# PReLU of a block pair: two loops over the pair, or one loop that alternates ScalarE and VectorE

## The chip, the cores and the metric

The kernel runs on one core of a Trainium2 chip. The metric is the device time of one execution, in microseconds. Three runs of the kernel before gave 373.78, 374.03 and 374.71 us, so the median is 374.03 us. The profiled execution took 374.39 us, and the span that its trace covers is 372.4 us. The TensorE clock was granted in full in it (mean 1.00).

## The reference

Two stages are chained. The first is a state-space scan (Mamba-2 SSD) over 4 batches, 8 heads and 768 tokens in chunks. Its result, laid out as 3072 tokens by 256 features, is the input of a feed-forward block with a PReLU:

```python
h = x @ w_in                                            # 3072 x 256 by 256 x 2048
g = np.maximum(h, 0.0) + alpha * np.minimum(h, 0.0)     # alpha: one slope per column, 2048
return (g @ w_out).astype(np.float32)                   # 3072 x 2048 by 2048 x 256
```

Everything is float32. The slope is a value per hidden feature, and hidden features lie on partitions in the kernel, so PReLU of a tile is two elementwise instructions with a scalar per partition. The first writes `alpha * h`; the second writes `max(s * h, that)` over it, where `s` is 1 or -1 (the sign is minus for slopes over 1, and is taken out again through the weights).

## The kernel before, in words

**Tiling.** The 3072 tokens are six groups of 512. A group's tokens come from two pairs of SSD chunks (`ssm`, `pair`, lines 416 to 637), which end in the tile `xT`. Group 0 goes through the feed-forward block plainly, tile by tile, while weights arrive (`hidden`, `output`, lines 643 to 688). Groups 1 to 5 use a seven-product scheme for a 2 by 2 block product instead of eight products, on both matrix products. One step of it is a *quad* (`quad`, line 760): four tiles of 128 hidden features, that is two row blocks of two tiles each, by 512 tokens, that is two column blocks of 256. There are four quads in a group, so twenty in all, from about 82 us to 361 us of the span.

**A quad.** Two PSUM tiles of one bank each, `A` and `Y` (name `hp`, pool `ps_h`, two buffers), receive the seven products of `x` with `w_in`. `first` (line 770) makes one product as two matmuls, one per half of the bank: half `p` = 0 and half `p` = 1. Between the products ScalarE and VectorE copy and add, so that four blocks result: `g12` from `Y` (line 799), `g22` from `c22` in SBUF (lines 800 and 802), `g21` from `A` (line 808), and `g11` from `Y` again (line 812). Each block is 128 partitions by two halves of 256, and PReLU is applied half by half because the two halves have different slopes. GpSimd then forms the block differences `tc_` (line 806) and `ta`, `tb`, `td` (line 815) from the four blocks. The copy of line 801 writes `m1` back into `Y` before the last product is added to it.

**The order around it.** The order of the work is written out by hand: nothing is rescheduled. `after(j)` is called between the steps of a quad and puts other work there for TensorE: the seven output products of the quad before (`product`, line 736), and the stages of the next SSD pairs (`ssm`). Every engine takes its instructions in the order in which the source issues them. Waits between engines are put in from the tiles that instructions read and write. For a PSUM bank an instruction also waits for another engine that uses any part of the bank; for an SBUF tile only for what touches the same part.

**The SSD pairs.** The pairs of groups 2 to 5 are worked in the quads of the group before. In every quad with `z` = 0 or 2 of groups 1 to 4 (eight quads, called *even* below), `after(13)` places the products of `products_bc` (line 563). They are eight matmuls into four PSUM tiles, `r` = 0 to 3, first for chunk 0 and then for chunk 1. Tiles `r` = 2 and `r` = 3 are taken by `spare` from the pool `ps_h`, so they take over the banks of `A` and `Y` of the running quad. VectorE multiplies them into `dec` (line 606). Between `g21` and `g11` VectorE also has the state updates (`states`, line 532) in these quads; ScalarE has a copy of the state (line 529) or a copy for the group's result (line 834) there in some of them.

The next quad takes the two `hp` buffers over in the same way: its `A` follows the old `A` (or tile `r` = 2), its `Y` the old `Y` (or tile `r` = 3).

Of the kernel before, what the change touches and what calls it, by code (L numbers as in the profile page):

```python
# [12 lines left out]
ALU = mybir.AluOpType  # L13
# [9 lines left out]
def kernel(  # L23
# [25 lines left out]
    nc = tc.nc  # L49
# [250 lines left out]
    s_mul = const.tile([P, NF], F32, name="s_mul")  # L300
    s_alpha = const.tile([P, NF], F32, name="s_alpha")
# [449 lines left out]
    def prelu(o, h, z, i, by=(nc.scalar, nc.vector)):  # L751

        fs = [slice(4 * z + 2 * p + i, 4 * z + 2 * p + i + 1) for p in range(2)]
        for p in range(2 if nc.scalar in by else 0):
            nc.scalar.mul(o[:, p], h[:, p], s_alpha[:, fs[p]])  # L755
        for p in range(2 if nc.vector in by else 0):
            nc.vector.scalar_tensor_tensor(out=o[:, p], in0=h[:, p], scalar=s_mul[:, fs[p]],  # L757
                                           in1=o[:, p], op0=ALU.mult, op1=ALU.max)

    def quad(g, z, after):  # L760

# [35 lines left out]
        first(Y, lambda q: s4[:, q], b22)  # L797
        g12, g22, g21, g11 = (tile_of(gp, "gt", "gt") for i in range(4))
        prelu(g12, Y, z, 0)
        prelu(g22, c22, z, 1, (nc.scalar,))  # L800
        nc.scalar.copy(out=Y, in_=m1)
        prelu(g22, c22, z, 1, (nc.vector,))
        after(7)
        after(8)
# [284 lines left out]
```

## Time and profile before

| | |
|---|---|
| median of three runs | 374.03 us |
| span of the trace | 372.4 us |
| TensorE busy | 365.4 us, 98% |
| VectorE busy | 243.1 us, 65% |
| GpSimd busy | 201.1 us, 54% |
| ScalarE busy | 179.7 us, 48% |
| line 755 on a PSUM half (ScalarE) | 120 instructions, mean 470 ns |
| line 757 on a PSUM half (VectorE) | 120 instructions, mean 479 ns |
| line 755 and 757 on an SBUF half | 40 each, mean 504 and 498 ns |

Busy time is the time in which an engine had at least one instruction in work. Where two instructions of one engine follow each other without a wait, the second starts before the end of the first is recorded, so a pair takes less than two single ones. The view in order of time merges such runs: it gives the start of the first, the time that the run covers, and the number of instructions; in brackets it gives the idle time before it and what ended that. Line numbers are those of the kernel before; in the kernel after, lines behind the change are one higher.

### The profile page before, as it was taken

The numbers are of one execution on the slowest core, as the hardware profiler recorded it, in microseconds if no ns is written. First come the engines' busy times: TensorE is split into PE (matmuls) and PEld (weight loads), VectorE is DVE, ScalarE is ACT, GpSimd is POOL, SyncE is SP. The second block draws the span as 40 slices with busy tenths as digits, with TensorE's granted clock in tenths as the row PEclk, the third lists the DMA queues.
The fourth block names the chain that finished last, engine by engine and source line by source line (L and its number), as shares of the span: only waits on it lengthen the run. The fifth ranks groups of instructions, "written<-read, shape, count | busy, mean of one in ns | idle before, by whom it ended". The sixth has DMA issues, their size and how long they took to land.

```text
span 372.4 us, 6183 instructions
## 1 busy us (share of the span) xinstructions
PE 365.4 (98%) x2223; PEld 295.1 (79%) x2223; DVE 243.1 (65%) x462; ACT 179.7 (48%) x384; POOL 201.1 (54%) x211
## 2 busy tenths in 40 slices
PE   8989999999999999999999999999999999999996
PEld 8766666578788888788788788788788788888884
DVE  7897979976448548738638847637848644643364
ACT  1647866435355355444444445445535525553541
POOL 4775565778929754724644525555445355264512
PEclk9999999999999999999999999999999999999999
DMA  7889999911176301005603703702801001001004
GB/s 147 181 151 322 276 284 202 181 31 58 48 136 112 72 3 56 2 0 79 134 3 61 151 2 54 159 0 45 167 2 29 2 0 23 8 0 30 1 0 85
DMA packets 121878, 30.71 MB, mean 82 GB/s; under 512 B 93736, under 2 KB 117752, under 8 KB 121848
## 3 DMA queue, kind: packets, MB, share of 16 engines
q1 hardware_dynamic: 116736, 29.74, 36.0%
q10 hardware_dynamic: 5112, 0.59, 1.1%
q8 instruction: 17, 0.28, 0.3%
q14 instruction: 13, 0.11, 0.1%
HBM read 26.98 MB, written 3.34 MB: 81 GB/s over the span
## 4 chain that ended last, share of the span: by engine, by line
PE 86%; DVE 10%; DMA 2%; issue 1%; ACT 1%; POOLq 0%; DVEq 0%; SPq 0%
PE hp L772 34%; PE bank L747 32%; PE bank L686 4%; DVE dec L438 3%; PE hp L648 2%; PE ss L629 2%; PE ss L570 2%; DMA rows<-in_a_dram 2%; DVE wr L239 1%; PE hp L270 1%; PE ss L622 1%; DVE dec L432 1%; PE hp L570 1%; DVE gt L652 1%; PE ss L520 1%; PE hp L663 1%
## 5 line engine op out<-in xcount | busy, mean ns | idle before, releaser
L815 POOL TENSOR_TENSOR gt<-gt 128x512 f32<-128x512 f32 x58 | 73.6, 1268 | 30.8 <-DVE gt L757 23.9
L757 DVE SCALAR_TENSOR_TENSOR gt<-hp,s_mul,gt 128x256 f32<-128x256 f32 x120 | 52.5, 479 | 46.9 <-ACT gt L755 45.9
L747 PE MATMUL bank<-gt,w_out 128*128 128x256 f32 x320 | 82.4, 382 | 0.0
L755 ACT ACTIVATE gt<-hp,s_alpha 128x256 f32<-128x256 f32 x120 | 50.3, 470 | 46.7 <-PE hp L772 32.5
L747 PEld LDWEIGHTS bank<-gt,w_out 128*128 128x128 f32 x320 | 60.1, 190 | 10.4 <-issue 2.3
L806 POOL TENSOR_TENSOR gt<-gt 128x512 f32<-128x512 f32 x20 | 25.4, 1270 | 78.8 <-DVE gt L757 78.8
L747 PE MATMUL bank<-gt,ws 128*128 128x256 f32 x240 | 58.3, 379 | 0.0
L747 PEld LDWEIGHTS bank<-gt,ws 128*128 128x128 f32 x240 | 45.1, 190 | 5.8
L438 DVE TENSOR_TENSOR_SCAN dec<-abc,bank 128x256 f32<-128x256 f32 x80 | 48.1, 660 | 0.0
L772 PE MATMUL hp<-xs,w_in 128*128 128x256 f32 x160 | 42.9, 390 | 0.0
L772 PE MATMUL hp<-xT,w_in 128*128 128x256 f32 x160 | 41.9, 384 | 0.0
L772 PE MATMUL hp<-xs,ws 128*128 128x256 f32 x160 | 41.1, 379 | 0.0
L791 DVE TENSOR_TENSOR hp<-hp,u 128x512 f32<-128x512 f32 x20 | 14.0, 700 | 39.8 <-ACT u L789 39.8
L780 ACT COPY m<-hp 128x512 f32<-128x512 f32 x20 | 11.7, 586 | 51.8 <-PE hp L772 51.8
L772 PEld LDWEIGHTS hp<-xs,w_in 128*128 128x128 f32 x160 | 28.7, 189 | 7.7 <-issue 3.0
L772 PEld LDWEIGHTS hp<-xs,ws 128*128 128x128 f32 x160 | 30.4, 190 | 4.1
L772 PEld LDWEIGHTS hp<-xT,w_in 128*128 128x128 f32 x160 | 29.7, 190 | 5.0 <-issue 1.4
L686 PE MATMUL bank<-w_out,gt 128*128 128x256 f32 x128 | 31.0, 384 | 0.0
L686 PEld LDWEIGHTS bank<-w_out,gt 128*128 128x128 f32 x128 | 23.7, 190 | 6.6 <-issue 3.7
L795 DVE TENSOR_TENSOR c<-hp,m 128x512 f32<-128x512 f32 x20 | 13.6, 681 | 19.3 <-PE hp L772 19.3
L648 PE MATMUL hp<-xT,w_in 128*128 128x512 f32 x48 | 22.8, 597 | 0.4 <-DVE gt L652 0.2
L789 ACT COPY u<-hp 128x512 f32<-128x512 f32 x20 | 11.7, 585 | 22.5 <-PE hp L772 22.5
(156 smaller groups left out, 555.4 us busy)
## 6 DMA issues: line engine op xcount, KB each, us to landing
abc<-z SPq DMA_DIRECT2D x20, 512.0 KB, 5.0
raw<-in_moe_w_in_dram SPq DMA_DIRECT2D x8, 512.0 KB, 5.0
raw<-in_moe_w_out_dram SPq DMA_DIRECT2D x8, 512.0 KB, 6.9
xt<-in_x_dram SPq DMA_DIRECT2D x24, 128.0 KB, 2.8
out_dram<-o_sb SPq DMA_DIRECT2D x32, 64.0 KB, 1.9
nat<-in_B_dram SPq DMA_DIRECT2D x22, 64.0 KB, 3.3
nat<-in_C_dram SPq DMA_DIRECT2D x22, 64.0 KB, 2.7
ap<-pf SPq DMA_DIRECT2D x11, 128.0 KB
```

Of the source, the lines that this page charges most:

```text
L438: nc.vector.tensor_tensor_scan(out=dv[:, k, hs], data0=abc[k][:, hs], data1=ident_p[0], initial=0.0, op0=ALU.mult, op1=ALU.add)
L648: nc.tensor.matmul(hp, w_in[:, k, f * P : (f + 1) * P], xts[g][:, k], start=(k == 0), stop=(k == KC - 1))
L686: nc.tensor.matmul(pos[0][t // 2][:, t % 2], gt[:, t * Q : (t + 1) * Q], w_out[:, f], start=(f == 0 and t % 2 == 0), stop=(f == NF - 1), s ...
L747: nc.tensor.matmul(ms[g][i][:, h], w, blocks[g, z][n][:, p], start=(q == 0 and h == 0), stop=(q == NQ - 1), skip_group_check=True)
L755: nc.scalar.mul(o[:, p], h[:, p], s_alpha[:, fs[p]])
L757: nc.vector.scalar_tensor_tensor(out=o[:, p], in0=h[:, p], scalar=s_mul[:, fs[p]], in1=o[:, p], op0=ALU.mult, op1=ALU.max)
L772: nc.tensor.matmul(to[:, p], w(2 * z + p), b, start=start and p == 0, stop=True, skip_group_check=True)
L780: nc.scalar.copy(out=m1, in_=A)
L791: nc.vector.tensor_tensor(out=Y, in0=Y, in1=u2, op=ALU.add)
L795: nc.vector.tensor_tensor(out=c22, in0=A, in1=m5, op=ALU.add)
L806: nc.gpsimd.tensor_tensor(out=tc_, in0=g22, in1=g12, op=ALU.subtract)
L815: eng.tensor_tensor(out=o, in0=x0, in1=x1, op=ALU.subtract)
```

## The change

PReLU of a block was issued as two loops over the halves: both ScalarE instructions, then both VectorE instructions. It is now one loop: ScalarE and VectorE for half 0, then ScalarE and VectorE for half 1. The aim is that VectorE begins on half 0 when ScalarE has written that half, and need not wait until both are written. Where `prelu` is called for one engine alone (`g22`, lines 800 and 802), the instructions are as before.

```diff
     def prelu(o, h, z, i, by=(nc.scalar, nc.vector)):
 
         fs = [slice(4 * z + 2 * p + i, 4 * z + 2 * p + i + 1) for p in range(2)]
-        for p in range(2 if nc.scalar in by else 0):
-            nc.scalar.mul(o[:, p], h[:, p], s_alpha[:, fs[p]])
-        for p in range(2 if nc.vector in by else 0):
-            nc.vector.scalar_tensor_tensor(out=o[:, p], in0=h[:, p], scalar=s_mul[:, fs[p]],
-                                           in1=o[:, p], op0=ALU.mult, op1=ALU.max)
+        for p in range(2):
+            if nc.scalar in by:
+                nc.scalar.mul(o[:, p], h[:, p], s_alpha[:, fs[p]])
+            if nc.vector in by:
+                nc.vector.scalar_tensor_tensor(out=o[:, p], in0=h[:, p], scalar=s_mul[:, fs[p]],
+                                               in1=o[:, p], op0=ALU.mult, op1=ALU.max)
```

## The prediction, made before the changed kernel was run

> **What bounds the kernel now.** I read the busy shares first, then the list of waits, then one quad in order of time.
>
> ```profile
> PE 365.4 (98%) x2223; PEld 295.1 (79%) x2223; DVE 243.1 (65%) x462; ACT 179.7 (48%) x384; POOL 201.1 (54%) x211
> ```
>
> TensorE has 7 us without work in 372.4. It sets the end, so whatever makes it wait goes onto the time one for one. Nothing else is near its limit. So the change cannot gain by engine time; it acts only through what TensorE waits for.
>
> ```profile
> DVE gt L757 <- ACT gt L755: 45.9, 54, 1.2
> ...
> ACT hp L801 <- DVE gt L757: 5.0, 20, 0.5
> ```
>
> VectorE idles 45.9 us ahead of line 757, until ScalarE's line 755 is done. That is what the change aims at. TensorE hardly waits for line 757 by this list, but the list does not see all. Here is the second half of one even quad, in order of time:
>
> ```profile
> 236.24 0.84 ACT L755 ACTIVATE gt<-hp,s_alpha 128x256 f32<-128x256 f32 x2 [0.18 <-PE hp L772]
> ...
> 237.11 0.88 DVE L757 SCALAR_TENSOR_TENSOR gt<-hp,s_mul,gt 128x256 f32<-128x256 f32 x2 [0.94 <-ACT gt L755]
> ...
> 237.89 0.84 ACT L755 ACTIVATE gt<-hp,s_alpha 128x256 f32<-128x256 f32 x2 [0.66 <-PE hp L772]
> 237.91 0.34 DVE L532 SCALAR_TENSOR_TENSOR state<-state,ap,ss 128x128 f32<-128x128 f32 x1
> ...
> 238.76 0.88 DVE L757 SCALAR_TENSOR_TENSOR gt<-hp,s_mul,gt 128x256 f32<-128x256 f32 x2 [0.52 <-ACT gt L755]
> 239.45 0.19 PEld L570 LDWEIGHTS ss<-cz,bc 32*128 32x128 f32 x2 [0.33 <-issue]
> ...
> 239.46 0.18 PEld L570 LDWEIGHTS hp<-cz,bc 32*128 32x128 f32 x1
> ...
> 239.57 0.30 PEld L570 LDWEIGHTS hp<-cz,bc 32*128 32x128 f32 x2
> ```
>
> VectorE's pair for g11 ends at 238.76 + 0.88 = 239.64. The last row is two weight loads that cover 0.30 us; one lasts 0.184 (the median of these loads), so the second begins at 239.57 + 0.30 - 0.184 = 239.69, 0.05 after g11 is done. It is the first load for tile r = 3, which takes over the bank of Y. In the products of the first SSD pairs, at 10.9 us, the first loads for the four tiles stand 20 ns apart from first to last; here r = 3 comes 240 ns behind r = 0. So TensorE already waits 0.22 us for g11, inside a group in which other loads run, where the list of waits misses it. The same 242 to 247 ns stand in six of the other even quads. In the first, g11 ends at 95.00 for a reason of its own; r = 3 follows at 95.05, 560 ns behind r = 0, and the last load of the group is 315 ns later than in the others. So a later g11 moves the whole group, and TensorE takes its work in order.
>
> **What the skill says.** "PSUM — Partial Sum Buffer", section "PSUM bank collisions raise a hardware error", says that two engines must not access one bank in the same partitions at once, two readers included, and that software has to keep them apart. The trace agrees as far as it goes: in all 60 PReLUs on PSUM VectorE starts on the bank only after both ScalarE instructions, although its half 0 was ready earlier. The section "Engine vs sequencer instructions" of that page says that the queues of ScalarE and VectorE are strictly in order; the trace shows nothing against it. "Perfetto Trace Analysis", section "Optimizing Scalar/DVE Operations", says that about half of an instruction's latency is the write acknowledgement, which overlaps with the next instruction of the engine, and that breaking up instructions may end bubbles elsewhere. The first half of this agrees: two ScalarE halves take 0.84 us, one takes 0.47.
>
> **The change, part by part.** It adds and removes no instruction; the order on every engine is the same. Only waits change, as a comparison of the two built programs shows. *Removed:* VectorE's half 0 no longer waits for ScalarE's half 1. *Added:* ScalarE's half 1 waits for VectorE's half 0 (same bank), and VectorE's half 1 for ScalarE's half 1. The two engines cannot overlap on Y or A; they now hand the bank over three times instead of once. For g22 in SBUF nothing changes.
>
> The prices: one ScalarE half 0.465, one VectorE half 0.475 us (within 0.01 of the shortest and the median of their rows), the pairs 0.84 and 0.88. The handover from ScalarE to VectorE is 0.03 here (236.24 + 0.84 = 237.08 to 237.11) and up to 0.09 in other quads; I take 0.06. From VectorE to ScalarE, line 801 starts 0.09 after the end of line 757. Before: 0.84 + 0.06 + 0.88 = 1.78. After: 0.465 + 0.06 + 0.475 + 0.09 + 0.465 + 0.06 + 0.475 = 2.09. So one PReLU gets 0.31 longer, 0.25 to 0.40 with handovers of 0.04 and 0.09.
>
> Behind the waiting ScalarE half stand g22's two halves and the copy into Y; behind the waiting VectorE half stand the state updates of the SSD. So the delays add up along the quad. For the one shown: g12 starts at 233.64 as before; g12's VectorE ends at 235.73 (before 235.39). ScalarE's g22 halves follow its half 1, the copy into Y ends at 236.49 (before 236.07), and TensorE's last product loads its weights at 236.66: still in time. g21: ScalarE 236.40, VectorE 236.92, ScalarE 237.49, VectorE 238.01 to 238.49 (before 237.99). The state update (0.34), which waits in VectorE's queue, ends at 238.75 (before 238.25). g11: ScalarE's half 0 is done at 238.50, VectorE's half 0 runs 238.67 to 239.15 behind the state update, ScalarE's half 1 239.24 to 239.70, VectorE's half 1 239.76 to 240.24, where it was 239.64. That is 0.60 us, all of it on TensorE through r = 3.
>
> The same chain, with the other even quads' own instructions between g21 and g11, gives 1.1 (two state updates and a weight sum on VectorE), 0.8, 0.85, 0.9, 0.9, 0.6, 0.95 and 0.85: together 6.9 us. It is more than 0.31 each because a VectorE half 0 that comes late behind state updates now holds up ScalarE's half 1, which used to be long done.
>
> In the twelve other quads the next use of Y is the next quad's second product. Up to the sixteenth quad its loads start 0.8 us after g11 or later, against a delay of 0.3 to 0.4: nothing, hidden behind the output products. In the last groups the margin is 0.37 (337.61 to 337.98): with 0.05 to notice it, delays of 0.32 fit, and 0.5 in one with a copy between: 0.2 in all. The copy into Y, 0.42 later, has a margin of 0.5 in most quads and 0.35 in one: 0.1. At the end TensorE waits for g11 anyway: 0.3. The sum is 6.9 + 0.2 + 0.1 + 0.3 = 7.5 us, so 374.0 + 7.5 = 381.5. Handovers of 0.04 give 380.8 and of 0.09 give 382.8.
>
> **The rivals.** *Only the handovers:* if VectorE's state updates slip into its idle times so that nothing piles up, each even quad pays 0.31: 8 x 0.31 + 0.6 = 3.1, so 377.1. For it: VectorE is busy only 65%. Against: its queue is in order, and the updates stand between g21 and g11.
> *The pile goes further:* the margins of 0.37 and 0.5 that I count as just enough are not, and 0.1 to 0.2 is lost in the remaining twelve quads too, at both places: 8.8 + 12 x 0.2 = 11.2, so 385.2. For it: the margins are within 0.1 of the delays. Against: a stall at one place gives slack at the next.
> *Hidden:* TensorE's wait is covered by the group around it, and 374 to 375 stays. For it: the list of waits hardly shows TensorE behind line 757. Against: the 0.05 us between g11 and r = 3, in eight quads of eight.
> *Faster:* if the halves did overlap, g11 would come 0.4 us earlier and TensorE's 0.22 us in eight quads would go: 374.0 - 1.8 = 372.2. For it: that is the shape of a pipeline. Against: the added waits in the built program.
>
> **How the numbers follow.** The forecast of about 381.5 has 0.73, only the handovers 0.13, the longer pile 0.07, hidden 0.04, faster 0.03. The range of 377.0 to 384.5 takes in the first rival and the dearer handovers; outside are the hidden and faster cases and most of the long pile. Slower: 0.73 + 0.13 + 0.07 = 0.93; no change 0.04; faster 0.03.
>
> **What would show it.** In the changed kernel the pairs of lines 756 and 758 on `hp` should stand apart as single instructions in turn, each with a wait for the other engine: ScalarE should show a wait of around 0.6 us for VectorE some 60 times, where before it had none. In even quads the first load for r = 3 should stay 0.05 behind the end of g11 and be 0.8 to 1.3 us behind r = 0. Products and chain of the quads between should keep their lengths. I am wrong if r = 3 comes before g11's end, if ScalarE's and VectorE's halves overlap on one bank, or if the even quads grow by less than 0.4 us each.

## The result, and the profile after

The changed kernel took 380.03 us (median of 4 runs, 379.58 to 380.35) against 373.90 us for the kernel before (4 runs, 373.67 to 374.71). The ratio is 1.0159, with a 95% interval of 1.0140 to 1.0178. So the kernel got about 6.1 us slower; the forecast was 7.5 us, at 381.5 us.

The busy times of the kernel after are these:

```profile
PE 368.0 (97%) x2223; PEld 294.0 (78%) x2223; DVE 248.1 (66%) x462; ACT 182.0 (48%) x384; POOL 201.3 (53%) x211
```

No engine has more instructions than before. The span grew by 6.2 us (372.4 to 378.6). VectorE's and ScalarE's busy times grew by 5.0 and 2.3 us, although their instructions are the same: most single instructions no longer lie over each other's ends. (A ScalarE pair took 0.84 us, two single halves take 2 x 0.47; for VectorE it is 0.88 against 2 x 0.48.)

The list of waits of the kernel after (who waited for whom: total us, how often, the longest):

```profile
DVE gt L758 <- ACT gt L756: 50.2, 98, 0.7
...
ACT gt L756 <- DVE gt L758: 36.4, 60, 1.6
...
PEld hp L570 <- DVE gt L758: 5.6, 8, 1.3
```

The first row is the wait that the change aimed at. It has not shrunk: 50.2 us against 45.9. It is paid in 98 smaller pieces, since both halves wait now. The second row is new: 60 waits of 0.61 us on average, one for each of the 60 PReLUs on PSUM. The third row is where the time goes: TensorE's loads for the SSD products wait for VectorE's PReLU, eight times, once per even quad. Before, this wait was shown once, with 0.3 us, in the listing of line 570.

This is the same even quad as in the prediction, in order of time:

```profile
240.43 0.47 ACT L756 ACTIVATE gt<-hp,s_alpha 128x256 f32<-128x256 f32 x1
...
240.93 0.48 DVE L758 SCALAR_TENSOR_TENSOR gt<-hp,s_mul,gt 128x256 f32<-128x256 f32 x1 [0.40 <-ACT gt L756]
241.45 0.48 ACT L756 ACTIVATE gt<-hp,s_alpha 128x256 f32<-128x256 f32 x1 [0.55 <-DVE gt L758]
...
241.96 0.48 DVE L758 SCALAR_TENSOR_TENSOR gt<-hp,s_mul,gt 128x256 f32<-128x256 f32 x1 [0.54 <-ACT gt L756]
241.97 0.49 ACT L756 ACTIVATE gt<-hp,s_alpha 128x256 f32<-128x256 f32 x1
...
242.36 0.34 DVE L532 SCALAR_TENSOR_TENSOR state<-state,ap,ss 128x128 f32<-128x128 f32 x1
...
242.62 0.48 DVE L758 SCALAR_TENSOR_TENSOR gt<-hp,s_mul,gt 128x256 f32<-128x256 f32 x1
...
243.13 0.47 ACT L756 ACTIVATE gt<-hp,s_alpha 128x256 f32<-128x256 f32 x1 [0.67 <-DVE gt L758]
...
243.64 0.48 DVE L758 SCALAR_TENSOR_TENSOR gt<-hp,s_mul,gt 128x256 f32<-128x256 f32 x1 [0.54 <-ACT gt L756]
...
244.17 0.18 PEld L570 LDWEIGHTS hp<-cz,bc 32*128 32x128 f32 x1 [0.34 <-DVE gt L758]
```

Each half stands alone now. On one bank the engines take turns and never overlap: ScalarE 241.45 to 241.93, VectorE from 241.96. (241.96 and 241.97 do overlap: VectorE is on `A`, for g21, and ScalarE already on `Y`, for g11.) VectorE's half 0 of g11 begins at 242.62 behind the state update, so ScalarE's half 1, which used to be done by then, starts at 243.13. g11 ends at 243.64 + 0.48 = 244.12, and the first load for r = 3 follows at 244.17, 0.05 us later as before.

Where the 6.2 us of the span went can be read from the length of each quad. A quad starts with its first matmul of line 772 (773 in the kernel after): the eleventh, which is the one shown, runs from 227.27 to 241.72 before and from 231.35 to 246.20 after. Lengths are in us:

| quads, in order | before | after | longer by | g11's end, counted from the quad's start, later by |
|---|---|---|---|---|
| 1 (even) | 15.77 | 16.79 | 1.02 | 1.02 |
| 3 (even) | 14.29 | 15.25 | 0.96 | 0.97 |
| 5 (even) | 14.51 | 15.13 | 0.62 | 0.62 |
| 7 (even) | 14.45 | 15.23 | 0.78 | 0.78 |
| 9 (even) | 14.30 | 14.98 | 0.68 | 0.68 |
| 11 (even) | 14.45 | 14.85 | 0.40 | 0.40 |
| 13 (even) | 14.51 | 15.36 | 0.85 | 0.86 |
| 15 (even) | 14.23 | 14.85 | 0.62 | 0.62 |
| the eleven others but the last, each | 12.17 to 14.49 | the same within 0.01 | 0.00 | 0.27 to 0.32 |
| 20, with the end of the kernel | 22.95 | 23.18 | 0.23 | 0.27 |

The even quads give 5.96 us and the end 0.23, which is the growth of the span (sums here and below are of unrounded lengths; the rounded ones give 5.93). Each even quad grows by what g11 is late, to 0.01 us. In the others g11 is late too, by 0.3, and nothing follows from it: the loads of the next quad's second product still start 0.05 us or more behind the end of g11.

### The profile page after: what moved, and what is told of

Read it like the earlier page. It is cut to its first block, busy times and chain, and to the rows that moved or that the text cites. A ratio compares the mean times of both kernels' runs of the same rounds, so it can differ in the third digit from the quotient of the medians.

```text
span 378.6 us, 6134 instructions
## 1 busy us (share of the span) xinstructions
PE 368.0 (97%) x2223; PEld 294.0 (78%) x2223; DVE 248.1 (66%) x462; ACT 182.0 (48%) x384; POOL 201.3 (53%) x211
## 4 chain that ended last, share of the span: by engine, by line
PE 70%; DVE 15%; ACT 7%; DMA 3%; issue 2%; POOL 2%; SPq 0%; POOLq 0%; DVEq 0%; ACTq 0%
PE hp L773 28%; PE bank L747 26%; ACT gt L756 5%; DVE gt L758 5%; DVE dec L438 3%; PE bank L686 3%; PE ss L629 2%; PE hp L648 2%; PE hp L570 2%; DMA rows<-in_a_dram 2%; PE ss L622 1%; DVE wr L239 1%; DVE gt L652 1%; PE hp L663 1%; DVE state L532 1%
## 5 line engine op out<-in xcount | busy, mean ns | idle before, releaser
L758 DVE SCALAR_TENSOR_TENSOR gt<-hp,s_mul,gt 128x256 f32<-128x256 f32 x120 | 58.0, 483 | 51.3 <-ACT gt L756 50.2
L756 ACT ACTIVATE gt<-hp,s_alpha 128x256 f32<-128x256 f32 x120 | 56.6, 474 | 66.8 <-DVE gt L758 36.4
```

## The experiments

Theory: TensorE loses time because g11 leaves the bank of `Y` later and tile r = 3 takes this bank over. Main rival: the added waits and handovers cost time where they stand, so spread over all PReLUs. The time ahead of the first quad differs by up to 0.8 us between profiles of kernels that are alike there (81.4 to 82.2 us), so growth summed over the quads is given beside the times.

**Two PReLUs of three alternate (e1).** `prelu` gets a switch; g12 and g21 alternate, g11 keeps two loops.

```diff
-        prelu(g12, Y, z, 0)
+        prelu(g12, Y, z, 0, turns=True)
...
-        prelu(g21, A, z, 1)
+        prelu(g21, A, z, 1, turns=True)
```

> Only g12 and g21 alternate; g11 has two loops, as before. Theory (what counts is when g11 leaves the bank of Y, since r = 3 takes it over): g21 is late by about 0.4 us, g11's pair then keeps its own length and is late only where work between g21 and g11 had no slack: 0.4 in the first even quad, about 0.3 in four, 0.1 or less in the rest, 2.3 us together, 376.2 us; no loss at the end. Rival (each added wait costs the same, wherever it stands): two of three PReLUs, so two thirds of 6.1 us, 378.0 us.

Measured: 375.47 us against 373.96, ratio 1.0041 (1.0026 to 1.0056), 1.5 us. The quads grew by 1.69 us: 0.38, 0.12, 0.35, 0.15, 0.40, 0.02, 0.21 and 0.06 in the even ones, 0 in the others and at the end. The theory was 0.6 to 0.8 too high and the rival of 378.0 is out.

**The third PReLU alone alternates (e2).**

```diff
-        prelu(g11, Y, z, 0)
+        prelu(g11, Y, z, 0, turns=True)
```

> Only g11 alternates; g12 and g21 have two loops, as before. Theory: every even quad pays at least g11's own lengthening of 0.26 us, and where state updates hold up VectorE's half 0 it pays up to 0.6: 2.9 us, and 0.2 at the end of the kernel: 377.0 us. Rival (each added wait costs the same): one third of 6.1 us, 375.9 us.

Measured: 376.76 us, ratio 1.0073 (1.0056 to 1.0090), 2.7 us by the ratio. The even quads grew by 0.63, 0.32, 0.27, 0.41, 0.31, 0.27, 0.48 and 0.27, the end by 0.23: 3.2 us. The theory's 377.0 (2.9 and 0.2 us) lies in the interval of 376.1 to 377.3, the rival's 375.9 just below it. One PReLU of three costs more than the other two together: it is the one that stands last before the takeover. The list of waits tells the two kernels apart, first with g12 and g21 alternating, then with g11:

```profile
PEld hp L570 <- DVE gt L758: 1.3, 4, 0.6
```
```profile
PEld hp L570 <- DVE gt L758: 2.8, 8, 0.9
```

The parts do not add up to the whole: 1.69 + 2.96 = 4.65 us in the even quads against 5.96. The missing 1.3 us stand in five quads: 0.52 in the third, 0.29 in the fifteenth, 0.22 in the seventh, 0.16 in the thirteenth and 0.11 in the eleventh. In these five VectorE's half 0 of g11 starts 0.16 to 0.55 us after ScalarE's half 0 is done, behind a late state update, and ScalarE's half 1 waits for it. This fits a late g21 that makes the state updates late, which matters more when g11 alternates too. Part of the third quad's share is something else: one VectorE half of g22 took 1.08 us in e1 and 1.36 in the changed kernel.

In the fifth and the ninth quad the two parts do add up, to 0.62 and 0.71 against 0.62 and 0.68, and the delay comes through ScalarE's own queue. This is g21's and g11's ScalarE work in the fifth quad, first before (g11 alone), then after:

```profile
151.78 0.84 ACT L755 ACTIVATE gt<-hp,s_alpha 128x256 f32<-128x256 f32 x2 [0.38 <-PE hp L772]
```
```profile
153.32 0.47 ACT L756 ACTIVATE gt<-hp,s_alpha 128x256 f32<-128x256 f32 x1 [0.55 <-DVE gt L758]
153.69 0.36 ACT L835 COPY sa<-bank 128x256 f32<-128x256 f32 x1
153.95 0.28 ACT L529 COPY state<-ss 128x128 f32<-128x128 f32 x1
154.10 0.50 ACT L756 ACTIVATE gt<-hp,s_alpha 128x256 f32<-128x256 f32 x1
```

ScalarE's half 1 of g21 waits for VectorE, the two copies stand behind it, and g11's half 0 follows them instead of waiting for its product. Counted from the quad's start it is 0.33 us late here and 0.39 in the ninth quad. VectorE follows it 0.03 and 0.05 us after its end, so in these two quads VectorE's state updates are not what makes g11 late.

**Without the takeover (e3 and e4).** Tile r = 3 of the SSD pairs of groups 2 to 5 is left out with its multiplication, so the result lacks these parts, in the kernel after (e3) and in the kernel before (e4).

```diff
-                    .rearrange("p (k h t) -> p k h t", k=2, h=2) for r in range(4)}
+                    .rearrange("p (k h t) -> p k h t", k=2, h=2) for r in range(3 if fine else 4)}
...
-                for r in range(4):
+                for r in range(3 if fine else 4):
...
-        for i, r in enumerate(r for r in ((2, 3, 0, 1) if fine else ...
+        for i, r in enumerate(r for r in ((2, 0, 1) if fine else ...
```

> The changed kernel without the products for tile r = 3 of the SSD pairs of groups 2 to 5, and without their multiplication into dec (two of the eight heads of these pairs are left out of the masking). Nothing then takes over the bank of Y inside an even quad. Theory: the loss goes but for the 0.2 us at the end; this kernel lies 0.2 to 0.6 us over the kernel before with the same products left out, near 372.5 us. Rival (the loss comes from the waits themselves, spread over the quads): it stays 6 us over that kernel, near 378 us.

> The kernel before with the same products and multiplications left out (tile r = 3 of the SSD pairs of groups 2 to 5). Theory: the wait of 0.22 us in each of seven even quads and 0.54 us in the first goes, 1.8 to 2.1 us less, near 372.0 us. Rival (that wait is covered by the group around it): 373.9 us, no change.

Measured: 371.57 us for the changed kernel (ratio 0.9934, 0.9919 to 0.9949) and 371.44 us for the kernel before (0.9937, 0.9917 to 0.9956). The difference of 6.1 us is gone: 0.13 us are left between the medians and 0.35 in the quads' lengths, where 0.2 to 0.6 was expected. (Both times lie under the forecasts of 372.5 and 372.0, by 0.9 and 0.6 us.) The changed kernel of e3 still has every added wait:

```profile
DVE gt L758 <- ACT gt L756: 50.1, 98, 0.7
...
ACT gt L756 <- DVE gt L758: 36.4, 60, 1.6
```

and g11 still ends 0.40 to 1.02 us later in its even quads. It costs next to nothing there: after an even quad no product of the next quad starts sooner than 0.7 us behind it. This settles it against the rival: the added waits alone cost 0.12 us in eight quads, and the takeover of the bank turns them into time. The quads of e4 are 0.55 us shorter in the first even one and 0.23 in the seven others, 2.16 us in all, so TensorE's wait at r = 3 was a cost in the kernel before too. In e3 the ninth and the fifteenth quad lack 0.09 and 0.03 us of this: there TensorE waits 0.26 and 0.20 us for the copy into `Y`, against 0.17 in five other even quads. The end costs 0.23.

**TensorE's order changed, in both kernels (e7 and e8).** Half of one output product (the part of product 3 for the second half, p = 1) goes from before g21's product to just ahead of the SSD products, in seven even quads. Nothing is left out.

```diff
-                product(*divmod(NZ + i - 1, NZ), places[j])
+                split = places is with_gram and places[j] == 3
+                product(*divmod(NZ + i - 1, NZ), places[j], (0,) if split else (0, 1))
+            if i and j == 12 and places is with_gram:
+                product(*divmod(NZ + i - 1, NZ), 3, (1,))
```

> The kernel before (PReLU in two loops), with the second matmul pair of output product 3 moved, in seven even quads, from the place after g12's product to the place ahead of the SSD products. The last product of Y, and with it g11, comes up to 0.43 us sooner, and TensorE has 0.43 us more to do between it and r = 3. Theory: the 0.22 us wait at r = 3 goes in seven quads, less about 0.3 us in all where the last product now waits for the copy into Y: 1.2 us less, 372.7 us. Rival (the wait moves to another place in the quad): no change.

> The same move in the changed kernel. Theory: there g11's end in even quads follows the ScalarE and VectorE chain of the alternating halves and no longer TensorE's last product, so an earlier product brings little: 0.1 us in each of seven quads at most, 379.3 to 380.0 us. Rival (TensorE's order sets g11 in both kernels): the full 0.4 us in seven quads, 377 us.

Measured: 372.75 us from the kernel before (14 runs; before 373.57 in 23 runs), ratio 0.9975 (0.9966 to 0.9984): 0.9 us less, where 1.2 was expected. From the changed kernel 379.52 us, ratio 1.0154 (1.0139 to 1.0170), no different from 1.0159. In e7 g11 ends 0.27 to 0.43 us sooner in the seven quads, and TensorE no longer waits at r = 3: its first load stands 20 ns behind r = 0 in all seven. The row below is from the eleventh quad; its two loads are the first ones of r = 2 and r = 3. Before, that row held the load of r = 2 alone (239.46 0.18, x1).

```profile
238.60 0.19 PEld L570 LDWEIGHTS hp<-cz,bc 32*128 32x128 f32 x2
```

The seven quads are 1.0 us shorter, since five of them lose part of the 0.23: the list now has seven waits of TensorE for the copy into `Y`, 1.4 us together, where the kernel before has none. In e8 the quads keep the lengths of the changed kernel (the third by 0.93 instead of 0.96), and the wait goes to the copy instead:

```profile
PEld hp L773 <- ACT hp L802: 3.3, 7, 0.6
...
PEld hp L570 <- DVE gt L758: 2.9, 5, 1.3
```

In the changed kernel the first row stood at 1.0 us and the second at 5.6. So there the alternating halves set the length of an even quad, and TensorE's order no longer does.

**A faster version (e9).** e7, and in the first even quad one weight sum on VectorE is put behind g11.

```diff
-                 (0, 10): ((wqt, out_sums, 0, 3, nc.vector),), (1, 2): ((wi, in_sums, 4, 1),),
+                 (0, 12): ((wqt, out_sums, 0, 3, nc.vector),), (1, 2): ((wi, in_sums, 4, 1),),
```

> The version with the half product moved in the kernel before, and in the first even quad the one weight sum that stands on VectorE between g21 and g11 put behind g11. Theory: g11 of that quad ends 0.32 us sooner, and its 560 ns at r = 3 shrink to about 240 ns: 0.3 us less than with the half product alone, 372.4 us, the fastest of all. Rival (the first quad waits for something else): as with the half product alone.

Measured: 372.51 us (10 runs), ratio 0.9968 (0.9957 to 0.9978): faster than both kernels. The first quad is 0.32 us shorter, as expected, and its first load for r = 3 stands 244 ns behind r = 0 instead of 560 in the kernel before and in e7. The two times of e7 and e9 lie within each other's intervals; the 0.32 us is seen in the traces only.

## Why the prediction was right

**The bound and the path.** TensorE set the end, and each microsecond that it waited was added. The path through g11, the bank of `Y` and r = 3 was right: the 0.05 us between g11's end and r = 3 stood in all eight quads of both kernels, and taking the takeover away (e3 against e4) took nearly the whole difference away. The list of waits had missed it; what gave it away was the spacing of the first loads for the four tiles, 20 ns in one place and 240 in the other. So *hidden* is out. *Faster* is out too: the finer order ended no idle time of TensorE, and its wait at r = 3 grew.

**The waits.** ScalarE waits 60 times, 0.61 us each, for VectorE: "around 0.6 us some 60 times" was forecast. No two halves of the two engines overlap on one bank in any of the 60 PReLUs.

**The pile-up.** Only the handovers, 0.31 us a quad, was the nearest rival. The even quads grew by 0.40 to 1.03, so it is out, though the eleventh stands right at the limit that the prediction set (0.40). e1 and e2 show the pile: two shares of 1.69 and 2.96 us that are worth 5.96 together. The prediction gave one cause for it, VectorE's state updates. In the fifth and the ninth quad the delay came through ScalarE's queue instead, with its copies. The rival of a pile that goes further is out as well: outside the even quads only the end grew.

**Sizes.** The term for the even quads was too large: 5.96 us against 6.9. The handovers were priced at 0.06 and 0.09 us and took 0.034 and 0.035 (medians). The 0.09 came from the copy of line 801, which has a separate semaphore instruction ahead of it; the PReLU halves of the changed kernel have none. In the quad that the prediction works out, the eleventh, g21 ended 0.37 us later and not 0.50, and g11 0.40 and not 0.60. One PReLU of an undisturbed quad therefore got 0.27 us longer and not 0.31 (g11 of the eighteenth quad: 1.75 us before, 341.82 to 343.84 = 2.02 after). In the third quad the delay was above the forecast (0.96 against 0.8), and that hid a part of the excess in the others: there one VectorE half of g22 takes 1.3 to 1.4 us in both kernels, and in the changed one g21 took 2.40 us behind it, against 2.01 in the other even quads. The first load for r = 3 came 0.65 to 1.59 us behind r = 0, where 0.8 to 1.3 was named; the eleventh quad lies below and the first above. In the last quads the margin of 0.37 held, by 0.05 us in one, with delays of 0.27 to 0.32, so the 0.2 us forecast there was 0. The copy into `Y` was forecast at 0.1; in the changed kernel it added nothing that the quads' lengths show, though TensorE's loads waited 1.0 us for it, because the wait at r = 3 took it up; in e3, without that wait, it shows as 0.12. The end was 0.23 instead of 0.3.

**What stays open.** Why that one half of g22 takes 1.1 to 1.5 us, in the third quad of every kernel here, was not tried. The 1.3 us that e1 and e2 leave over were read from their traces and that of the changed kernel; no run moved the state updates or ScalarE's copies alone. Alternating halves that lie in two banks was not run either.

## What to carry to other kernels

In none of the 60 PReLUs on PSUM, before or after, do ScalarE and VectorE work on one bank at the same time. There, alternating them half by half makes no pipeline but a chain with three handovers, and a PReLU of 1.75 us takes 2.02. So before splitting work between two engines, ask which buffer the parts share (parts in two banks were not tried here). Look for what takes a buffer over next: here a producer's lateness of 0.3 to 1.0 us cost time only where something waited for its buffer or its result, and the list of waits did not show a wait that other work of the same group covered. A queue in order passes a small delay on when the next instruction in it is one that another engine waits for. In the quads between, the delays of g12 and g21 were absorbed, and g11 was late by its own 0.27 to 0.32 us; in the even quads, with state updates or copies in the queues between g21 and g11, 0.40 to 1.03 us arrived.

## What the runs showed of the hardware

The handover between ScalarE and VectorE came in two sizes here. In the changed kernel the waiting instruction has no separate semaphore instruction (one that only waits) ahead of it, and it starts 33 to 36 ns after the end of the other: 60 of 60 waits of line 756 for line 758, and 60 of 60 of VectorE's half 1 for ScalarE's. With such an instruction ahead of it in the queue, the handover mostly takes 88 to 103 ns: in the kernel before, 19 of the 20 copies of line 801, each of which has one, and 24 of the 26 PReLUs on PSUM whose first VectorE half has one. Of the 34 PReLUs without one, 30 took under 40 ns. The two go together in these traces; no run added or removed such an instruction alone.
